# Turning C and B by VectorE's 32x32 transposes for three of six chunks

## The chip, the cores and the metric

One core of one Trainium2 chip runs the whole program. The metric is device time in microseconds (us) of one execution. Engines are named as the profile names them: PE is TensorE, PEld its weight loads, DVE VectorE, ACT ScalarE, POOL GpSimd, and SP the engine that issues all DMAs here. All data are float32.

## The reference, cut to what matters

A state-space scan in chunks (4 batches, 8 heads, 768 tokens, head size 32, state size 16) is followed by a feed-forward block with a hard-swish.

```python
for c in range(nc):                                   # chunks of tokens
    cum = np.cumsum(la, axis=-1)                      # la = log of the decay a
    L = np.exp(cum[:, :, :, None] - cum[:, :, None, :]) * causal
    M = np.einsum('bhin,bhjn->bhij', Cc, Bc) * L
    y_intra = np.einsum('bhij,bhjd->bhid', M, xc)
    y_inter = np.einsum('bhin,bhnd->bhid', Cc, state) * np.exp(cum)[:, :, :, None]
    y[:, :, sl] = y_intra + y_inter
    Bx = np.einsum('bhjn,bhjd->bhjnd', Bc, xc) * decay_from_j[:, :, :, None, None]
    state = decay_full[:, :, None, None] * state + np.sum(Bx, axis=2)
# y as (3072, 256), then
h = y @ w_in                                          # 256 x 2048
g = h * np.clip(h + 3.0, 0.0, 6.0) / 6.0
return g @ w_out                                      # 2048 x 256
```

Both products of C, with B and with the state, contract over the state size n. On TensorE the contracted dimension lies on the partitions, so C and B, which come from memory with n innermost, are needed with n on the partitions. Getting them there is called turning.

## The kernel before

The kernel uses chunks of 128 tokens, six in all. Stage k = 0 to 5 computes the feed-forward block of chunk k while it prepares the scan of chunk c = k + 1 and loads chunk `ahead` = k + 2. The instructions of each engine run in the order in which the program writes them (a manual schedule), and SP's queue too. A tile that reuses a buffer waits until the readers of the old content are done.

Stages 1 to 5 have two halves on TensorE:

- The first product (y times `w_in`) runs in steps s = 0 to 7. Each step issues `early`, `lead` of the next step, `last` of the previous one and `middle` (all recorded at L490). ACT and DVE fetch the banks `odd` and `even`, form the ramp (L524, L529) and leave the result in `gT`. The function `lead` ends with an ACT copy (L503) and the DVE copy `up` (L504), and `middle` with two DVE additions (L516, L517). POOL sums quarters of `gT` (`g_sums`, L585) after s = 2, 4, 6 and at the start of the second half.
- The second product (`gT` times `w_out`, L599) is a chain of 14 units, i = 0 to 13, in two rounds t = 0 and 1. They collect in two banks, `oa` and `ob`, and DVE combines them (L624 after unit 10, L634 and L635 after unit 12, L640 after unit 13 for t = 1; L644 to L646 after unit 7 for t = 0). Between the units the scan of the next chunk is placed: `scores` (products of C and B at L376, times L on DVE at L384) after units 2 and 4, `results` (`mix` on TensorE at L400, L409, L417, then `keep`, which copies y on ACT at L432 and updates the state on DVE) after units 4 and 7, `sum_y` (DVE, L487) after unit 7, and `lead` of the next stage after unit 12. ACT's exponentials of chunk `ahead` (L312, and `from_start`, L315, for the table `eto`) run after units 2 to 6.

Turning a chunk takes two calls of `turn`, each for two batches. In stages 1 to 4 they stand in the first product, after steps s = 3 and s = 5. Each call has four TensorE transposes of 128x128 into one PSUM bank `t_ps` (L343), an ACT copy that takes B out as `bT` (L347), a DVE product that takes C out twice, masked by the head's parity, as `cT` (L359), and a DVE product with the decay from the chunk's start, `eto`, as `csT` (L365). In stage 0 chunk 1 is turned, and chunk 0 before that.

In `load`, SP brings C and B of a chunk as tokens by heads (L85) and x (L92), three issues at the start of a stage. `rows` brings the cumulated log decays for chunk `ahead` + 1 after unit 7: four issues for L (L247), which POOL masks in `conceal` (L303), and eight for `eto` (L253), one for each head, which land in 16 partitions each. B by tokens is also multiplied by the decay to the chunk's end (`ends`, POOL, L323). The scan's decay from chunk to chunk is applied by `carry` (POOL, L331).

Of the kernel before, what the change touches and what calls it, by code (L numbers as in the profile page):

```python
# [8 lines left out]
FP32 = mybir.dt.float32  # L9
# [3 lines left out]
AF = mybir.ActivationFunctionType  # L13
ALU = mybir.AluOpType
# [6 lines left out]
def kernel(  # L21
# [23 lines left out]
    nc = tc.nc  # L45
    P = 128
# [3 lines left out]
    NC = S // P  # L50
# [25 lines left out]
    a_sb = pre[:G, 0:2].rearrange("g t i -> g (t i)")[:, :S]  # L76
    nc.sync.dma_start(out=a_sb, in_=a.rearrange("b h s -> (b h) s"))

    loaded = {}

    def load_bc(c):
        sl = slice(c * P, (c + 1) * P)
        bc = loads.tile([P, 2, NB * NH, N], FP32, name="bc")
        for j, src in enumerate((C, B)):
            nc.sync.dma_start(  # L85
                out=bc[:, j], in_=src[:, :, sl, :].rearrange("b h s n -> s (b h) n"))
        loaded[c] = bc

    def load_x(c):
        sl = slice(c * P, (c + 1) * P)  # L90
        xt = loads.tile([P, NB * NH, D], FP32, name="xt")
        nc.sync.dma_start(out=xt, in_=x[:, :, sl, :].rearrange("b h s d -> s (b h) d"))  # L92
        loaded[c] = loaded[c], xt

    w_in = const.tile([P, NK, DF], FP32, name="w_in")
    w_sum = const.tile([P, NF // 2, P], FP32, name="w_sum")
# [152 lines left out]

    def load_eto(c):  # L250
        eto = att.tile([P, NB, P], FP32, name="eto")
        for h in range(NH):
            nc.sync.dma_start(  # L253
                out=eto[h * N:(h + 1) * N],
                in_=cum_d[c, h:NB * NH:NH].unsqueeze(0).to_broadcast([N, NB, P]))
        etos[c] = eto

    cum_n = const.tile([P, NC, G], FP32, name="cum_n")
# [58 lines left out]
    def ends(c, b):  # L317

        if c < NC - 1:
            if b == 0:  # L320
                bss[c] = att.tile([P, G, N], FP32, name="bs")
            hs = slice(b * NH, b * NH + NH)
            nc.gpsimd.tensor_tensor(  # L323
                out=bss[c][:, hs], in0=loaded[c][0][:, 1, hs],
                in1=decays_of(c, b)[:, :, P - 1:P].to_broadcast([P, NH, N]), op=ALU.mult)

    def carry(c):

        if c < NC - 1:
# [2 lines left out]
                out=tmps[c], in0=states[c - 1],  # L332
                in1=etos[c][:, :, P - 1:P].to_broadcast([P, NB, 2 * D]), op=ALU.mult)

    def turn(c, p):


        bc, xt = loaded[c]
        pool, tag = (ps, "f") if c < 2 else (ps_o, "o")
        t_ps = pool.tile([P, 4, P], FP32, name="t_ps", tag=tag)  # L340
        for k in range(4):
            j, b = k // 2, 2 * p + k % 2
            nc.tensor.transpose(  # L343
                out=t_ps[:, k],
                in_=bc[:, j, b * NH:(b + 1) * NH].rearrange("s h n -> s (h n)"), identity=ident)
        bT = att.tile([P, 2, P], FP32, name="bT")
        nc.scalar.copy(out=bT, in_=t_ps[:, 2:4])  # L347
        if c == 1 and p == 0:
            from_start(c)
            carry(c)  # L350
            for b in range(NB):
                ends(c, b)
        cT = att.tile([P, 2, 2, P], FP32, name="cT")
        if c == 1 or (c, p) == (0, 1):
            for t in range(2):
                nc.scalar.activation(
                    cT[:, :, t], t_ps[:, 0:2], AF.Copy, scale=parity[:, t:t + 1])
        else:
            nc.vector.tensor_tensor(  # L359
                out=cT, in0=t_ps[:, 0:2].unsqueeze(2).to_broadcast([P, 2, 2, P]),  # L360
                in1=parity.unsqueeze(1).unsqueeze(3).to_broadcast([P, 2, 2, P]), op=ALU.mult)
        csT = None
        if c:
            csT = att.tile([P, 2, P], FP32, name="csT")
            nc.vector.tensor_tensor(  # L365
                out=csT, in0=t_ps[:, 0:2], in1=etos[c][:, 2 * p:2 * p + 2], op=ALU.mult)
        bTs[c, p] = bT, cT, csT

    def scores(c, bs):

        bT, cT, csT = bTs[c, bs[0] // 2]
        cbs = [ps.tile([P, 2, 2, P], FP32, name="cb", tag="f") for q in range(NQ)]
        for b in bs:
            for q in range(NQ):
                rows = slice(32 * q, 32 * q + 32)
                nc.tensor.matmul(  # L376
                    out=cbs[q][:, b % 2].rearrange("j h i -> j (h i)"), lhsT=bT[rows, b % 2],
                    rhs=cT[rows, b % 2].rearrange("n t i -> n (t i)"), start=(b == bs[0]),
                    stop=True, tile_position=(32 * q, 0), skip_group_check=True)
        in_pair = slice(bs[0] % 2, bs[-1] % 2 + 1)  # L380
        L = Ls[c, bs[0] // 2][:, in_pair]
        for q in range(NQ):
            hs = slice(2 * q, 2 * q + 2)
            nc.vector.tensor_tensor(  # L384
                out=L[:, :, hs], in0=L[:, :, hs], in1=cbs[q][:, in_pair], op=ALU.mult)

    def mix(c, bs):


        xt = loaded[c][1]  # L390
        if bs[0] % 2 == 0:
            y_pss[c] = [ps_y.tile([P, 4, P], FP32, name=f"y{u}", tag=f"y{u}") for u in range(NK)]
        y_ps = y_pss[c]
        if c:

            for b in bs:
                csT = bTs[c, b // 2][2]
                for q in range(NQ):
                    rows, d0 = slice(32 * q, 32 * q + 32), 2 * D * (q % 2)
                    nc.tensor.matmul(  # L400
                        out=y_ps[q // 2][d0:d0 + 2 * D, b % 2], lhsT=states[c - 1][rows, b],
                        rhs=csT[rows, b % 2], start=(b == bs[0]), stop=True,
                        tile_position=(32 * q, d0), skip_group_check=True)
        for b in bs:
            L = decays_of(c, b)
            for u in range(NK):
                for q in range(HU):
                    h = HU * u + q
                    nc.tensor.matmul(  # L409
                        out=y_ps[u][32 * q:32 * q + 32, b % 2], lhsT=xt[:, b * NH + h],  # L410
                        rhs=L[:, h], start=(c == 0), stop=True, tile_position=(0, 32 * q),
                        skip_group_check=True)
        if c < NC - 1:
            for b in bs:
                for q in range(NQ):
                    hs = slice(b * NH + 2 * q, b * NH + 2 * q + 2)
                    nc.tensor.matmul(  # L417
                        out=y_ps[0][32 * q:32 * q + 32, 2 + b % 2, 0:2 * D],
                        lhsT=bss[c][:, hs].rearrange("s h n -> s (h n)"),
                        rhs=xt[:, hs].rearrange("s h d -> s (h d)"),  # L420
                        start=True, stop=True, tile_position=(0, 32 * q), skip_group_check=True)
# [232 lines left out]
    def rows(c):  # L654
        for b in range(NB):
            load_decay(c, b)
        load_eto(c)
# [91 lines left out]
    for k in range(NC):  # L749
# [56 lines left out]
        for s in range(NJ):  # L806
            early(k, s)
            if s == 0:
                if ahead < NC:
                    load(ahead)  # L810
                if c < NC:
                    carry(c)
            if s < NJ - 1:
                lead(k, s + 1)
            if s:
                last(k, s - 1)
                ramp(k, 2 * s - 2, evens[k, s - 1])
            middle(k, s)
            if s:
                times_ramp(k, 2 * s - 2, evens[k, s - 1])  # L820
            ramp(k, 2 * s + 1, odds[k, s])
            times_ramp(k, 2 * s + 1, odds[k, s])
            if s in (1, 3) and ahead < NC:
                conceal(ahead, s - 1)
                conceal(ahead, s)
            if s in (3, 5) and c < NC:
                turn(c, s // 4)
            if s in (2, 4, 6):
                g_sums(k, s - 2)
        for i, _ in enumerate(out_units(k)):  # L830
            if i == 0:
                s = NJ - 1
                last(k, s)
                ramp(k, 2 * s, evens[k, s])
                times_ramp(k, 2 * s, evens[k, s])
                g_sums(k, s - 1)
                if k == 1:
                    next(sums)
            if c < NC:
                if i in (2, 4):  # L840
                    if i == 4:
                        results(c, 0)
                    scores(c, ((0, 1), (2, 3))[i // 4])
                if ahead < NC and i in (2, 3, 5, 6):
                    decay_ends(ahead, {2: 0, 3: 1, 5: 2, 6: 3}[i])
                    if i == 6:
                        from_start(ahead)
                if i == 7:
                    results(c, 1)
                    sum_y(c)  # L850
                    if ahead + 1 < NC:
                        rows(ahead + 1)
                if i == 12:
                    lead(c, 0)

# [29 lines left out]
```

## Time and profile before

| | |
|---|---|
| median of 8 runs | 370.8 us (369.96 to 371.91) |
| the profiled execution | 370.13 us, of it 368.4 us span |
| granted TensorE clock, mean | 0.999 |
| PE busy | 360.4 us, 2893 instructions |
| DVE busy | 228.9 us, 448 instructions |
| ACT busy | 190.2 us, 414 instructions |
| POOL busy | 134.5 us, 134 instructions |
| TensorE transposes into `t_ps` (L343) | 48, 273 ns in the record |
| `bT` copies (L347, ACT) | 12, 366 ns |
| `cT` on DVE (L359) | 9, 685 ns |
| `csT` on DVE (L365) | 10, 417 ns |
| C issues (L85), 256 KB | 6, 5.4 us to landing |
| B issues (L85), 256 KB | 6, 7.7 us to landing |
| `eto` issues (L253), 32 KB | 40, 5.1 us to landing |

The span runs from the first to the last instruction; the execution's own time is a little longer. Busy time of PE is that of pipelined instructions whose ends are modelled, so the distance of the starts of two neighbours says more than the duration of one. A group's line gives line of code, engine, operation and tiles (out<-in), then count, busy time and mean time of one. In an order of time, a line begins with the start in us from the span's start and the busy us; what stands in brackets at its end is the idle time before it and what ended that.

### The profile page before, as it was taken

Reading aid. Unit: us, or ns where it says so; the run is one execution under the profiler, and the core shown is the slowest. Engines: PE = TensorE matmul, PEld = TensorE weight load, DVE = VectorE, ACT = ScalarE, POOL = GpSimd, SP = SyncE. Lnnn points to the kernel's source line nnn. Section 1 sums busy time; section 2 is a strip of 40 time slices with the busy share of each in tenths; the row PEclk is TensorE's granted clock in tenths of the full one; section 3 lists DMA queues with packets and bytes.
Section 4 is the critical chain, followed back from the end, with each engine's and each line's share of the span. In section 5 each row is a group of like instructions: output and inputs, shape, how many; then the busy total and the mean of one; then the engine's idle time right before and its main releaser. Section 6 shows DMA issues by size and latency. Waiting matters only on the chain.

```text
span 368.4 us, 7275 instructions
## 1 busy us (share of the span) xinstructions
PE 360.4 (98%) x2893; PEld 306.5 (83%) x2893; DVE 228.9 (62%) x448; ACT 190.2 (52%) x414; POOL 134.5 (37%) x134
## 2 busy tenths in 40 slices
PE   7899999999999999999999999999999999999996
PEld 3564468778888999888899888999888989888996
DVE  7779999894896632786452688343488342488111
ACT  5867878765674831674750575570466100366100
POOL 1200020631499412099512088600058800057800
PEclk9999999999999999999999999999999999999999
DMA  9968999703790036900027930000000000000000
GB/s 165 201 228 181 186 355 119 240 5 81 237 113 3 2 117 195 114 6 2 3 68 223 106 34 0 2 24 8 28 3 1 2 2 30 28 1 2 2 28 28
DMA packets 86689, 29.21 MB, mean 79 GB/s; under 512 B 75456, under 2 KB 81248, under 8 KB 86656
## 3 DMA queue, kind: packets, MB, share of 16 engines
q1 hardware_dynamic: 86656, 28.76, 38.2%
q8 instruction: 22, 0.36, 0.5%
q14 instruction: 11, 0.09, 0.1%
HBM read 25.53 MB, written 3.23 MB: 78 GB/s over the span
## 4 chain that ended last, share of the span: by engine, by line
PE 82%; DVE 8%; ACT 6%; DMA 2%; issue 1%; SPq 0%; ACTq 0%
PE even L490 19%; PE ob L599 17%; PE oa L599 17%; PE odd L490 14%; PE cb L376 4%; PE y L409 3%; PE o L540 3%; DVE gT L529 2%; DVE wm L178 2%; ACT we L175 2%; PE y L400 2%; DMA raw<-in_moe_w_in_dram 2%; ACT L L312 1%; ACT L L298 1%; PE t_ps L343 1%; DVE w_out L191 1%
## 5 line engine op out<-in xcount | busy, mean ns | idle before, releaser
L585 POOL TENSOR_TENSOR s<-gT 128x512 f32<-128x512 f32 x20 | 26.4, 1320 | 104.0 <-DVE gT L529 104.0
L490 PE MATMUL even<-ts,w_sum 128*128 128x256 f32 x160 | 48.2, 383 | 0.0
L524 ACT ACTIVATE gT<-odd,half 128x512 f32<-128x512 f32 x40 | 27.5, 687 | 35.5 <-DVE odd L517 35.5
L503 ACT COPY even<-odd 128x512 f32<-128x512 f32 x40 | 23.0, 575 | 43.0 <-PE odd L490 42.0
L312 ACT ACTIVATE L<-L,cum_n 128x128 f32<-128x128 f32 x144 | 43.2, 392 | 2.1 <-POOL L L303 2.1
L490 PE MATMUL odd<-yT,w_in 128*128 128x256 f32 x160 | 41.1, 379 | 0.0
L384 DVE TENSOR_TENSOR L<-L,cb 128x512 f32<-128x512 f32 (+1 forms) x56 | 30.3, 605 | 17.2 <-PE cb L376 17.2
L599 PE MATMUL oa<-w_out,gT 128*128 128x128 f32 x320 | 39.3, 278 | 0.0
L599 PEld LDWEIGHTS oa<-w_out,gT 128*128 128x128 f32 x320 | 38.1, 192 | 1.4 <-issue 0.2
L303 POOL TENSOR_SCALAR_AFFINE_SELECT L<-L 128x1024 f32<-128x1024 f32 x18 | 20.1, 1131 | 49.7 <-DMA L<-cum_d 49.6
L599 PE MATMUL ob<-w_out,s 128*128 128x128 f32 x320 | 37.8, 276 | 0.0
L599 PEld LDWEIGHTS ob<-w_out,s 128*128 128x128 f32 x320 | 36.5, 192 | 1.3 <-issue 1.3
L490 PEld LDWEIGHTS even<-ts,w_sum 128*128 128x128 f32 x160 | 29.9, 190 | 5.3 <-ACT up L510 1.5
L529 DVE SCALAR_TENSOR_TENSOR gT<-gT,odd 128x512 f32<-128x512 f32 x40 | 27.5, 687 | 9.9 <-ACT gT L524 9.8
L490 PEld LDWEIGHTS odd<-yT,w_in 128*128 128x128 f32 x160 | 30.1, 190 | 3.9
L524 ACT ACTIVATE gT<-even,half 128x512 f32<-128x512 f32 x40 | 27.8, 695 | 4.4 <-PE even L490 4.4
L529 DVE SCALAR_TENSOR_TENSOR gT<-gT,even 128x512 f32<-128x512 f32 x40 | 27.2, 679 | 4.4 <-ACT gT L524 4.4
L599 PE MATMUL ob<-t,gT 128*128 128x128 f32 x240 | 29.7, 277 | 0.0
L599 PEld LDWEIGHTS ob<-t,gT 128*128 128x128 f32 x240 | 28.0, 192 | 1.3 <-issue 1.3
L540 PE MATMUL o<-w_out,gT 128*128 128x256 f32 x128 | 28.9, 381 | 0.0
L504 DVE COPY up<-odd 128x256 f32<-128x256 f32 x40 | 16.9, 423 | 18.3 <-ACT even L503 14.4
L448 PE MATMUL h<-yT,w_in 128*128 128x512 f32 x64 | 27.7, 594 | 0.0
(110 smaller groups left out, 629.7 us busy)
## 6 DMA issues: line engine op xcount, KB each, us to landing
L<-cum_d SPq DMA_DIRECT2D x18, 512.0 KB, 6.8
raw<-in_moe_w_in_dram SPq DMA_DIRECT2D x4, 1024.0 KB, 8.5
raw<-in_moe_w_out_dram SPq DMA_DIRECT2D x4, 1024.0 KB, 8.8
xt<-in_x_dram SPq DMA_DIRECT2D x6, 512.0 KB, 8.6
out_dram<-res SPq DMA_DIRECT2D x20, 128.0 KB, 1.7
bc<-in_C_dram SPq DMA_DIRECT2D x6, 256.0 KB, 5.4
bc<-in_B_dram SPq DMA_DIRECT2D x6, 256.0 KB, 7.7
eto<-cum_d SPq DMA_DIRECT2D x40, 32.0 KB, 5.1
```

Of the source, the lines that this page charges most:

```text
L303: nc.gpsimd.affine_select(out=L, in_=L, pattern=[[0, NH], [1, P]], compare_op=ALU.is_ge, fill=-1e5, base=0, channel_multiplier=-1)
L312: nc.scalar.activation(L[:, h], L[:, h], AF.Exp, bias=cum_n[:, c, g:g + 1])
L384: nc.vector.tensor_tensor(out=L[:, :, hs], in0=L[:, :, hs], in1=cbs[q][:, in_pair], op=ALU.mult)
L448: nc.tensor.matmul(out=h.rearrange("p r i -> p (r i)"), lhsT=w_in[:, j, f * P:(f + 1) * P], rhs=yTs[k][:, j].rearrange("p b i -> p (b i)") ...
L490: nc.tensor.matmul(out=bank[:, r], lhsT=lhsT, rhs=rhs, start=start, stop=True, skip_group_check=True)
L503: nc.scalar.copy(out=even, in_=odd[:, 1:2].to_broadcast([P, 2, 2 * P]))
L504: nc.vector.tensor_copy(out=up[:, 1], in_=odd[:, 0])
L524: nc.scalar.activation(gTs[k][:, f], h.rearrange("p r i -> p (r i)"), AF.Relu, bias=half, scale=1.0 / 6.0)
L529: nc.vector.scalar_tensor_tensor(out=g, in0=g, scalar=1.0, in1=h.rearrange("p r i -> p (r i)"), op0=ALU.min, op1=ALU.mult)
L540: nc.tensor.matmul(out=o[:, b % 2], lhsT=gTs[0][:, f, b * P:(b + 1) * P], rhs=w_out[:, f], start=(f == 0 and b % 2 == 0), stop=True, skip_ ...
L585: nc.gpsimd.tensor_tensor(out=o, in0=p_, in1=q_, op=op)
L599: nc.tensor.matmul(out=bank[:, slot], lhsT=lhs[:, j], rhs=rhs[:, j], start=(clear and j == 0), stop=True, skip_group_check=True)
```

## The change

For chunks 3, 4 and 5 (`TURN = 3`), C and B are loaded a second way. Each partition holds one pair of heads and one group of four tokens, and its elements lie as head of the pair, batch, token of the group, state index. This takes eight issues of 32 KB for each of C and B, one for each batch and head of a pair. A block of 32 partitions and 32 elements then is 32 token groups by (head, state index), so a 32x32 transpose puts head and state index on the partitions and the tokens along the free dimension. The function `turn_all` turns the whole chunk by two such transposes on DVE, masks C twice by parity (two scalings of 128x512) and multiplies it by `eto`. It stands after unit 9 of the second product, for chunk `ahead`, so in stages 1, 2 and 3. The calls of `turn` in stages 2, 3 and 4 fall away. B by tokens is still loaded, for `ends`; C by tokens is not loaded for these chunks.

The tiles `bT`, `cT` and `csT` now hold a whole chunk, in one buffer each where there were two. The pair tiles of C and B share the two buffers of the old C tile.

For all chunks, `load_eto` has four issues, one for each batch, over all 128 partitions, instead of eight over 16 partitions each.

```diff
     def load_bc(c):
         sl = slice(c * P, (c + 1) * P)
-        bc = loads.tile([P, 2, NB * NH, N], FP32, name="bc")
-        for j, src in enumerate((C, B)):
-            nc.sync.dma_start(
-                out=bc[:, j], in_=src[:, :, sl, :].rearrange("b h s n -> s (b h) n"))
-        loaded[c] = bc
+        def tokens_first(src, **where):
+            t = loads.tile([P, NB * NH, N], FP32, **where)
+            nc.sync.dma_start(out=t, in_=src[:, :, sl, :].rearrange("b h s n -> s (b h) n"))
+            return t
+
+        def pairs_first(src):
+            t = loads.tile([P, 2, NB, 4, N], FP32, name="pairs", tag="bc")
+            for b in range(NB):
+                for h in range(2):
+                    nc.sync.dma_start(
+                        out=t[:, h, b].rearrange("s a n -> s (a n)"),
+                        in_=src[b, h:NH:2, sl, :].rearrange("h (s a) n -> h s (a n)", a=4))
+            return t
+
+        if c < TURN:
+            bcs[c] = [tokens_first(C, name="C", tag="bc")]
+        Bs[c] = tokens_first(B, name="B")
+        if c < TURN:
+            bcs[c].append(Bs[c])
+        else:
+            bcs[c] = [pairs_first(C), pairs_first(B)]
...
     def load_eto(c):
         eto = att.tile([P, NB, P], FP32, name="eto")
-        for h in range(NH):
+        for b in range(NB):
             nc.sync.dma_start(
-                out=eto[h * N:(h + 1) * N],
-                in_=cum_d[c, h:NB * NH:NH].unsqueeze(0).to_broadcast([N, NB, P]))
+                out=eto[:, b],
+                in_=cum_d[c, b * NH:(b + 1) * NH].unsqueeze(1).to_broadcast([NH, N, P]))
         etos[c] = eto
...
+    def turned(c):
+        if c not in bTs:
+            bTs[c] = [att.tile([P, 2, 2, P], FP32, name="bT", bufs=1),
+                      att.tile([P, 2, 2, 2, P], FP32, name="cT", bufs=1),
+                      att.tile([P, 2, 2, P], FP32, name="csT", bufs=1) if c else None]
+        return bTs[c]
...
+    def turn_all(c):
+
+        bT, cT, csT = turned(c)
+        for t, out_ in zip(bcs[c], (csT, bT)):
+            nc.vector.transpose(
+                out=out_.rearrange("r p b (s a) -> r (p b) a s", a=4),
+                in_=t.rearrange("s t b a n -> s (b a) t n"))
+        for t in range(2):
+            nc.vector.tensor_scalar(
+                out=cT[:, :, :, t].rearrange("r p b i -> r (p b) i"),
+                in0=csT.rearrange("r p b i -> r (p b) i"), scalar1=parity[:, t:t + 1],
+                scalar2=None, op0=ALU.mult)
+        nc.vector.tensor_tensor(
+            out=csT, in0=csT, in1=etos[c].rearrange("r (p b) i -> r p b i", p=2), op=ALU.mult)
...
-            if s in (3, 5) and c < NC:
+            if s in (3, 5) and c < TURN:
                 turn(c, s // 4)
...
+                if i == 9 and TURN <= ahead < NC:
+                    turn_all(ahead)
                 if i == 12:
                     lead(c, 0)
```

More of the change, by code (lines that the diff above doesn't have):

```diff
@@ L77 @@
     nc.sync.dma_start(out=a_sb, in_=a.rearrange("b h s -> (b h) s"))
-    loaded = {}
+    Bs, bcs, xts = {}, {}, {}
+    TURN = 3
     def load_bc(c):
         sl = slice(c * P, (c + 1) * P)
-        bc = loads.tile([P, 2, NB * NH, N], FP32, name="bc")
-        for j, src in enumerate((C, B)):
-            nc.sync.dma_start(
-                out=bc[:, j], in_=src[:, :, sl, :].rearrange("b h s n -> s (b h) n"))
-        loaded[c] = bc
+        def tokens_first(src, **where):
[17 more added lines that the diff above has]
+            bcs[c] = [pairs_first(C), pairs_first(B)]
     def load_x(c):
         sl = slice(c * P, (c + 1) * P)
-        xt = loads.tile([P, NB * NH, D], FP32, name="xt")
-        nc.sync.dma_start(out=xt, in_=x[:, :, sl, :].rearrange("b h s d -> s (b h) d"))
-        loaded[c] = loaded[c], xt
+        xts[c] = loads.tile([P, NB * NH, D], FP32, name="xt")
+        nc.sync.dma_start(out=xts[c], in_=x[:, :, sl, :].rearrange("b h s d -> s (b h) d"))
     w_in = const.tile([P, NK, DF], FP32, name="w_in")
@@ L323, in ends @@
             nc.gpsimd.tensor_tensor(
-                out=bss[c][:, hs], in0=loaded[c][0][:, 1, hs],
+                out=bss[c][:, hs], in0=Bs[c][:, hs],
                 in1=decays_of(c, b)[:, :, P - 1:P].to_broadcast([P, NH, N]), op=ALU.mult)
@@ L333, in carry @@
                 in1=etos[c][:, :, P - 1:P].to_broadcast([P, NB, 2 * D]), op=ALU.mult)
+    def turned(c):
[4 more added lines that the diff above has]
+        return bTs[c]
     def turn(c, p):
-        bc, xt = loaded[c]
+        bT, cT, csT = turned(c)
         pool, tag = (ps, "f") if c < 2 else (ps_o, "o")
@@ L344, in turn @@
                 out=t_ps[:, k],
-                in_=bc[:, j, b * NH:(b + 1) * NH].rearrange("s h n -> s (h n)"), identity=ident)
-        bT = att.tile([P, 2, P], FP32, name="bT")
-        nc.scalar.copy(out=bT, in_=t_ps[:, 2:4])
+                in_=bcs[c][j][:, b * NH:(b + 1) * NH].rearrange("s h n -> s (h n)"),
+                identity=ident)
+        nc.scalar.copy(out=bT[:, p], in_=t_ps[:, 2:4])
         if c == 1 and p == 0:
@@ L352, in turn @@
                 ends(c, b)
-        cT = att.tile([P, 2, 2, P], FP32, name="cT")
         if c == 1 or (c, p) == (0, 1):
@@ L356, in turn @@
                 nc.scalar.activation(
-                    cT[:, :, t], t_ps[:, 0:2], AF.Copy, scale=parity[:, t:t + 1])
+                    cT[:, p, :, t], t_ps[:, 0:2], AF.Copy, scale=parity[:, t:t + 1])
         else:
             nc.vector.tensor_tensor(
-                out=cT, in0=t_ps[:, 0:2].unsqueeze(2).to_broadcast([P, 2, 2, P]),
+                out=cT[:, p], in0=t_ps[:, 0:2].unsqueeze(2).to_broadcast([P, 2, 2, P]),
                 in1=parity.unsqueeze(1).unsqueeze(3).to_broadcast([P, 2, 2, P]), op=ALU.mult)
-        csT = None
         if c:
-            csT = att.tile([P, 2, P], FP32, name="csT")
             nc.vector.tensor_tensor(
-                out=csT, in0=t_ps[:, 0:2], in1=etos[c][:, 2 * p:2 * p + 2], op=ALU.mult)
-        bTs[c, p] = bT, cT, csT
+                out=csT[:, p], in0=t_ps[:, 0:2], in1=etos[c][:, 2 * p:2 * p + 2], op=ALU.mult)
+    def turn_all(c):
+        bT, cT, csT = turned(c)
+        for t, out_ in zip(bcs[c], (csT, bT)):
[9 more added lines that the diff above has]
+            out=csT, in0=csT, in1=etos[c].rearrange("r (p b) i -> r p b i", p=2), op=ALU.mult)
     def scores(c, bs):
-        bT, cT, csT = bTs[c, bs[0] // 2]
+        bT, cT = (t[:, bs[0] // 2] for t in bTs[c][:2])
         cbs = [ps.tile([P, 2, 2, P], FP32, name="cb", tag="f") for q in range(NQ)]
@@ L387, in mix @@
     def mix(c, bs):
-        xt = loaded[c][1]
+        xt = xts[c]
         if bs[0] % 2 == 0:
@@ L396, in mix @@
             for b in bs:
-                csT = bTs[c, b // 2][2]
+                csT = bTs[c][2][:, b // 2]
                 for q in range(NQ):
```

## The prediction

> **What bounds the kernel now.** I read four views in this order: the busy shares of the page, busy time by stage, TensorE's order of time around the transposes, and VectorE's order of time where the new block goes.
>
> First a line of the page's first part, then two tables by stage. Their windows run from one "early" product of a stage to that of the next: stages k = 2, 3, 4, then k = 5 to the end. Each line has the length, then busy us and instruction count of each engine.
>
> ```profile
> PE 360.4 (98%) x2893; PEld 306.5 (83%) x2893; DVE 228.9 (62%) x448; ACT 190.2 (52%) x414; POOL 134.5 (37%) x134
> ```
>
> ```profile
> 145.72:202.74 57.02, 1.20 (x8) 1.00 (x8) 2.03 (x4) 0.73 (x2) 1.00 0.35 70
> ...
> 316.34:368.40 52.06, 0.00 (x0) 0.00 (x0) 0.00 (x0) 0.00 (x0) 0.99 0.04 13
> ```
>
> ```profile
> 202.74:259.76 57.02, 57.02 (x506) 51.70 (x505) 32.16 (x68) 29.13 (x72) 22.03 (x18) 1.00 0.25 30
> 259.76:316.34 56.58, 56.58 (x474) 51.05 (x473) 31.21 (x64) 19.25 (x39) 19.99 (x16) 1.00 0.03 11
> ```
>
> The columns are PE, PEld, DVE, ACT (and POOL), then granted clock, DMA share and GB/s. The second fence counts only instructions that touch `t_ps`; the third counts all. See: in stages 3 and 4 TensorE is busy for the whole stage at granted clock 1.00, and each stage still sends 8 transposes through it. DVE is busy for 56%. So work taken off TensorE there is time, and work given to DVE is free while it fits in a hole.
>
> TensorE in stage 4 (start, us, then instructions merged):
>
> ```profile
> 270.46 0.59 PE L490 MATMUL odd<-ts,w_in 128*128 128x256 f32 x2
> 270.89 0.59 PE L490 MATMUL even<-ts,w_sum 128*128 128x256 f32 x2
> 271.32 0.60 PE L343 MATMUL t_ps<-ident,bc 128*128 128x128 f32 x4
> 271.76 0.60 PE L490 MATMUL even<-yT,w_in 128*128 128x256 f32 x2
> ...
> 281.70 0.59 PE L490 MATMUL even<-ts,w_sum 128*128 128x256 f32 x2
> 282.25 0.70 PE L490 MATMUL even<-yT,w_sum 128*128 128x256 f32 x2
> ```
>
> See: the record says 273 ns for a transpose, but they are pipelined. What four of them cost is the distance of starts, 271.76 - 271.32 = 0.44 us. At the end of this first product the distance is 282.25 - 281.70 = 0.55 where it is 0.43 everywhere else. In stage 5, which turns nothing, the same pair stands 0.43 apart (337.40 and 337.83). So a stage that turns also has 0.12 us of wait.
>
> VectorE around the end of stage 2, the second place where the new block goes:
>
> ```profile
> 192.50 0.66 DVE L487 TENSOR_TENSOR yT<-yT 128x256 f32<-128x256 f32 x1
> 193.07 0.87 DVE L487 TENSOR_TENSOR ts<-yT,ts 128x256 f32<-128x256 f32 x2
> 196.56 0.42 DVE L624 TENSOR_TENSOR res<-oa,x 128x256 f32<-128x256 f32 x1 [2.61 <-DMA L<-cum_d]
> 200.13 0.42 DVE L634 TENSOR_TENSOR u<-ob,res 128x256 f32<-128x256 f32 x1 [3.15 <-PE ob L599]
> ```
>
> See: after `sum_y` (L487) DVE is idle 2.61 us, and 3.15 us more after `res`. The block stands between L487 and L624.
>
> **The change, part by part.** Sums are against the profiled execution: 370.13 us, of which 368.4 is span. The median of the runs shown is 370.8, so I add 0.67 at the end.
>
> *Transposes removed.* Chunks 3, 4 and 5 were turned in stages 2, 3 and 4, at steps s = 3 and 5: 2 x 0.44 = 0.88 us a stage. Check, by the same two groups of even products in the chain of waits: stage 4's first product takes 281.00 - 261.93 = 19.07, stage 5's 336.69 - 318.50 = 18.19; the difference is 0.88. Three stages: 2.64 us. The 0.12 wait is 0.36 over three stages. Bounds: nothing of it (it comes from something other than the turn), or all. I take 0.16, since stage 5 also lacks other work. Gain: 2.8 us.
>
> *Copies removed.* Per chunk, two `bT` copies on ACT (0.366 each), two `cT` (0.685) and two `csT` (0.417) on DVE. They are off TensorE's path, as the 0.88 shows: it is transposes alone. Their only worth is the 0.12 already taken.
>
> *The DVE block added, one per chunk in stages 1, 2 and 3 after unit 9.* Two 32x32 transposes of 128x512 f32 have no row. Nearest: a DVE operation over 128x512 f32, 0.682 (L384) to 0.687 (L529). Below: 0.41, the TENSOR_SCALAR over 32x512 f32 (L216), if a transpose also does two elements at a time. Above: 4 x 0.69 = 2.8 us, if a transpose of 4-byte elements with its writes 16 bytes apart took four passes. I take 0.69, as a single stream of 512 elements. Two scalings SBUF to SBUF: 0.41 each by L216. One product with `eto`: 0.69. Sum 2 x 0.69 + 2 x 0.41 + 0.69 = 2.9 us. Room: DVE is free at 193.95. What TensorE needs first is L624: it reads bank `oa`, which TensorE writes again at 200.79 (unit 13). So L624 must start by about 200.3, a room of 6.3 us. Behind it wait L634, L635 and `up` (L504, at 201.60), whose reader L516 comes at 205.45; these are looser. Cost: zero, hidden by units 10 to 12; without that cover it would be 2.9 x 3 = 8.7 us.
>
> Here a rule speaks against the change. Row: `yT<-yT` took 0.66 us at 192.50 in stage 2, while a POOL operation ran 192.19 to 192.87, and 0.43 in stage 3 with POOL idle. The Trainium skill, "SBUF — State Buffer", section "SBUF: two separate sides", says that VectorE (two SBUF inputs, or a two-port mode) and GpSimd hold a shared port pair exclusively for a whole instruction and the loser blocks. `conceal` (L303, 1.09 us each) runs at 195.65 and 198.28, inside the hole. By the row's 0.23 the block is 3.2; by the rule at most 2 x 1.09 more, so 5.1. Both are under 6.3. I take zero cost, but the margin by the rule is only 1.2 us.
>
> *Waits the block adds.* It needs `eto` after `from_start`: ACT ended that at 188.41, before `sum_y`. It overwrites `csT`, `cT` and `bT` of the chunk before, last read by the mix of unit 7 (TensorE, to 190.97), for which `sum_y` already waits. No added wait. Its result is first read a stage later.
>
> *Transfers of the pairs.* Per chunk of 3 to 5 the one C transfer goes, sixteen of 32 KB come, B by tokens stays. SP issues take 0.43 (C) or 0.30 to 0.86 (eto), so 16 cost 5 to 14 us of SP. In stages 2 and 3 they start near 146.6 and 203.6; SP's next work is at 190.08 in stage 2, so nothing waits behind but `x`, which is read a stage later. In stage 1 the B half reuses the buffer of chunk 2's C, so SP waits for that chunk's last transposes (106.74), with eight issues and `x` behind it; SP's next work is at 133.06. Landing: C and B of 256 KB land 5.4 and 7.7 us from issue, both inside 8.2. The Trainium skill, "DMA: Bandwidth & Descriptors", section "Why a DMA increments its semaphore by 16 and not by 1", says a transfer uses as many engines (16 at most) as divide the slowest dimension of both sides; here that is 4 heads against 128 partitions, so 4 engines. By the row: landed about 12 us after the first issue, with issue bound. By the rule: 4 x 8.2 = 33 us, plus some 3 us for B, so near 183 in stage 2, with DVE there at 193.95. In stage 1: half of it, 107 + 17 = 124 against 136.9. Zero by both; by the rule the cover is 11 to 13 us.
>
> *The decay table.* Eight issues become four, same bytes, chunks 1 to 5: SP is freed by 4 x 0.43 or more each time. The tightest reader is chunk 2's: issued 64.6 to 73.5, used on ACT at 86.64, and ACT's copy for the first lead follows it. Bounds: 0.3 us won (the one wait for a w_out load, 0.68, is in that stretch) or 0.5 lost. I take zero.
>
> *POOL.* The sum that unit 4 needs (`s2`) ends at 176.46; TensorE reads it at 178.72. With TensorE 1.0 us earlier, 1.3 us is left. Zero.
>
> Sum: 370.13 - 2.8 = 367.3, plus 0.67: 368.0.
>
> **Rivals.** *A: as summed.* 368.0, own range 367.0 to 369.4 (a DVE delay taking up to half the gain back).
>
> *B: the gain is eaten.* TensorE arrives early and waits for what did not move: POOL's sums, or ACT's exponentials before the `yT` copies (2.62 us idle at 191.03). Against it: 1.3 and 1.6 us of slack would be left. For it: POOL is slowed if DVE locks it out. Time: 370.0 to 371.5, near 370.8.
>
> *C: slower, the block holds DVE's queue.* Place: L624 behind the two transposes. If each takes 2.8 us the block is 5.6 + 1.5 = 7.1, and with `conceal` in the way 9.3. Past 6.3, each us is a us of TensorE at unit 13: 0.8 to 3.0 a stage. At 3.0 in stages 1 and 2 and 0.8 in stage 3: 6.8 - 2.8 = +4.0, so 374.8. It decides for slower once the block passes 6.3 + 2.8/3 = 7.2 us in every stage, which is 2.9 us a transpose (1.8 with the port). For it: no row of such a transpose. Against: every f32 DVE row over 512 elements from one stream is 0.4 to 0.7.
>
> *D: the change does not get TensorE off the turning, or the pairs come late.* The first would leave L343 at 48 instructions; the diff guards `turn` by `c < TURN`, so no. The second needs landings over 47 us.
>
> **How the numbers follow.** A 0.77, B 0.09, C with D's second half 0.14. A measurement here can tell about 0.3%, 1.1 us, from no change. A lies beyond it, so faster 0.77, same 0.09, slower 0.14. The range, 367.0 to 371.0, holds A and the nearer part of B.
>
> **What would show it.** L343 falls from 48 to 24. Stages 2, 3 and 4 fall from 57.02, 57.02, 56.58 to about 56.1, 56.1, 55.7, stages 1 and 5 staying within 0.2. A new DVE group of 6 transposes near 0.7 us starts at about 136.9 (stage 1), with L624 about 0.5 to 1.5 us later than now and L634 where it was relative to TensorE. L347 falls to 6. It would be wrong if PE shows idle at unit 13, or DVE waits for a transfer ahead of the transposes.

## The result and the profile after

The changed kernel takes 367.41 us in the median (367.04 to 369.2), the kernel before in the same comparison 370.38 us (369.9 to 372.1). The ratio is 0.9918, with a 95% interval of 0.9904 to 0.9932, so it is faster by about 3.0 us. The profiled execution took 368.2 us, of it 366.5 us span. One execution further down, of a kernel with VectorE's copies put back, ran at a granted clock of 0.56 and took 616.07 us, so its stages are not used; in the stages compared, k = 1 to 4, the clock was 1.00.

Here are the tables by stage of both kernels. Their windows run from one stage's first `early` product to the next's, for k = 1 to 5. Each line has the length, then busy us and count of PE, PEld, DVE, ACT and POOL, then clock, DMA share and GB/s. Before:

```profile
88.06:145.56 57.50, 57.47 (x506) 51.46 (x505) 33.61 (x69) 29.70 (x73) 29.68 (x27) 1.00 0.51 113
145.56:202.58 57.02, 57.02 (x507) 51.70 (x505) 32.39 (x68) 29.12 (x72) 26.51 (x25) 1.00 0.34 68
202.58:259.60 57.02, 57.02 (x506) 51.70 (x505) 32.16 (x68) 29.13 (x72) 22.03 (x18) 1.00 0.26 31
259.60:316.18 56.58, 56.58 (x475) 51.05 (x473) 31.21 (x64) 19.25 (x39) 19.99 (x16) 1.00 0.03 11
316.18:368.40 52.22, 48.92 (x334) 45.33 (x332) 22.89 (x48) 16.83 (x32) 19.95 (x16) 0.99 0.04 13
```

After:

```profile
88.87:146.33 57.46, 57.46 (x506) 51.46 (x505) 37.79 (x74) 29.69 (x73) 29.74 (x27) 1.00 0.47 118
146.33:202.35 56.02, 56.02 (x498) 50.92 (x497) 34.76 (x69) 28.57 (x70) 27.04 (x25) 1.00 0.34 76
202.35:258.37 56.02, 56.02 (x498) 50.92 (x497) 33.72 (x69) 28.58 (x70) 21.99 (x18) 1.00 0.21 34
258.37:313.95 55.58, 55.58 (x467) 50.27 (x466) 29.46 (x60) 18.70 (x37) 19.97 (x16) 1.00 0.03 11
313.95:366.50 52.55, 48.92 (x334) 45.33 (x332) 22.89 (x48) 16.84 (x32) 19.96 (x16) 1.00 0.04 13
```

Stages 2, 3 and 4, the three that no longer turn, are 1.00 us shorter each. Stage 1 still turns chunk 2 and is as before (57.50 and 57.46), although it now holds a DVE block too (DVE 37.79 us there). That makes 3.00 us, the whole gain by stages. These two spans differ by only 1.9 us, for two reasons. The last window is 0.3 us longer in the changed kernel. That is not chance: up to the last VectorE instruction stage 5 takes 48.96 us in both, and from there to the end it takes 3.5 to 3.6 us in every profile of a kernel with the new decay table, and 3.3 us in the two with the old one. So the table costs 0.2 to 0.3 us there; why is not shown. The other reason is that the profiled execution of the changed kernel came to stage 1 0.81 us later. This is not the change's: in a second profile of the changed kernel stage 1 began at 88.21. The late start shows in the first matmuls. Changed kernel, TensorE's order of time:

```profile
6.64 0.63 PE L311 MATMUL d<-less,split 128*128 128x512 bf16 x1
7.07 0.63 PE L308 MATMUL d<-split,pick 128*128 128x128 bf16 x4
```

The same place in the kernel before:

```profile
6.37 0.38 PE L292 MATMUL d<-less,split 128*128 128x512 bf16 x1
6.59 0.39 PE L289 MATMUL d<-split,pick 128*128 128x128 bf16 x4
```

The starts are 0.43 us apart in one and 0.22 in the other. Both executions begin with 0.43 (from 2.3 us on) and change to 0.22, one at 11.6 us and the other at 6.4. The trace's records of the granted clock begin just before, at 11.35 and at 5.68 us; for the time without a record the tables print 1.00, so a 1.00 in the first microseconds says nothing. The Trainium skill, "TensorE: Matmul & The Clock Gate", section "Wait — 56ns, not 53.3ns?", gives 426.7 ns for a 512-column matmul on a cold array and 215.7 on a warm one, and the distances agree. Since the moment of the change differs from execution to execution, I compare lengths of stages below, and times only where they say more.

VectorE at the end of stage 2, changed kernel:

```profile
192.84 0.87 DVE L524 TENSOR_TENSOR ts<-yT,ts 128x256 f32<-128x256 f32 x2
194.01 1.11 DVE L395 STREAM_TRANSPOSE csT<-pairs 128x512 f32<-128x512 f32 x1 [0.30 <-issue]
194.97 1.10 DVE L395 STREAM_TRANSPOSE bT<-pairs 128x512 f32<-128x512 f32 x1
195.90 0.81 DVE L399 TENSOR_SCALAR cT<-csT,parity 128x512 f32<-128x512 f32 x2
196.74 1.46 DVE L403 TENSOR_TENSOR csT<-csT,eto 128x512 f32<-128x512 f32 x1
198.12 0.41 DVE L661 TENSOR_TENSOR res<-oa,x 128x256 f32<-128x256 f32 x1
199.90 0.42 DVE L671 TENSOR_TENSOR u<-ob,res 128x256 f32<-128x256 f32 x1 [1.37 <-PE ob L636]
```

The block fills the hole of 2.61 us after `sum_y` and part of the next one. Of the 3.15 us that VectorE was idle before L634 (now L671), 1.37 us is left, and L671 still waits for TensorE. No transfer stands before the block.

### The profile page after: what moved, and what is told of

It reads as the page before. It is cut to its first block, busy times and chain, and to the rows that moved or that the text cites. A ratio compares the mean times of both kernels' runs of the same rounds, so it can differ in the third digit from the quotient of the medians.

```text
span 366.5 us, 7245 instructions
## 1 busy us (share of the span) xinstructions
PE 359.6 (98%) x2869; PEld 305.8 (83%) x2869; DVE 234.4 (64%) x451; ACT 189.2 (52%) x408; POOL 135.3 (37%) x134
## 4 chain that ended last, share of the span: by engine, by line
PE 80%; issue 10%; DMA 5%; SPq 3%; POOL 1%; DVE 0%; POOLq 0%
PE even L527 19%; PE ob L636 17%; PE oa L636 17%; PE odd L527 14%; PE o L577 3%; PE cb L413 3%; DMA B<-in_B_dram 3%; PE y L446 3%; DMA L<-cum_d 2%; PE y L437 2%; SPq L266 1%; SPq L112 1%; POOL L L322 1%; SPq L89 1%; POOL bs L342 1%
```

## The experiments

Stage lengths in us, k = 1 to 4. The changed kernel is the line to compare with.

| kernel | k = 1 | k = 2 | k = 3 | k = 4 | median time |
|---|---|---|---|---|---|
| before | 57.50 | 57.02 | 57.02 | 56.58 | 370.38 |
| changed | 57.46 | 56.02 | 56.02 | 55.58 | 367.41 |
| changed, again | 57.42 | 56.03 | 56.03 | 55.57 | 367.36 |
| transposes back | 57.51 | 56.90 | 56.91 | 56.45 | 370.05 |
| one transpose, all copies back | 57.41 | 57.18 | 57.18 | 56.73 | 371.25 |
| one transpose, DVE's copies back | 57.42 | 57.19 | 57.18 | 56.78 | 370.92 |
| copies from `odd` back | 57.46 | 58.24 | 58.24 | 57.86 | 374.22 |
| block with 4 transposes | 57.52 | 56.03 | 56.02 | 55.58 | 367.95 |
| block with 8 transposes | 60.15 | 58.65 | 58.35 | 55.58 | 375.02 |
| old decay table | 57.43 | 56.03 | 56.02 | 55.58 | 367.71 |
| chunk 2 too | 56.87 | 56.02 | 56.02 | 55.58 | 367.14 |
| chunk 2 too, split | 56.46 | 56.03 | 56.02 | 55.58 | 366.31 |

**Transposes back.** My theory was that the gain is TensorE's own time for the transposes. The rival was that it is the relief of VectorE and ScalarE.

```diff
             if s in (3, 5) and c < TURN:
                 turn(c, s // 4)
+            if s in (3, 5) and TURN <= c < NC:
+                idle_turn(c, s // 4)      # four TensorE transposes into t_ps, no reader
```

> The changed kernel with the 24 TensorE transposes put back in stages 2 to 4 after steps 3 and 5, into a bank that nobody reads (the result still comes from VectorE). Theory 1 (the gain is TensorE's own time, 0.44 us a call, and the other 0.12 us a stage was the copies' lag on VectorE and ScalarE): stages 2 to 4 at 56.90, 56.90, 56.46, the run about 2.6 us above the changed kernel, near 370.0. Theory 2 (the 0.12 too is TensorE's): stages at 57.02, 57.02, 56.58, 3.0 us above. Theory 3 (the gain is mainly VectorE's and ScalarE's relief in the first product): under 1 us above.

The first `early` products of its stages 4 and 5:

```profile
260.74 0.60 PE L536 MATMUL even<-yT,w_in 128*128 128x256 f32 x2
317.19 0.60 PE L536 MATMUL even<-yT,w_in 128*128 128x256 f32 x2
```

The stages grew by 0.88, 0.89 and 0.87 us, just theory 1. So four transposes cost 0.44 us of TensorE, and the other 0.12 us of a turning stage is there only when the copies are too. This does not say that the copies are worth no more than that.

**Copies back, first try.**

```diff
+            if s in (3, 5) and TURN <= c < NC:
+                idle_copies(c, k, s)      # ACT 128x256, DVE 128x512 and 128x256, out of odd
```

> The changed kernel with copies of the sizes of turn's put back in stages 2 to 4 after steps 3 and 5 (one 128x256 on ScalarE, one 128x512 and one 128x256 on VectorE, from a bank already there into an unread tile), without any TensorE work. Theory 1: only the 0.12 us a stage come back, stages at 56.14, 56.14, 55.70, the run 0.4 us above the changed kernel. Theory 2: nothing comes back, within 0.1 us. Theory 3: over 1.5 us above.

Each stage grew by 2.2 us. The run does not answer the question, because these copies wait as those of `turn` never did: ScalarE's for VectorE's `gT`, VectorE's for ScalarE's. They read the bank `odd` and write one tile; which of the two makes the waits is not shown. The waits of the tile of these copies:

```profile
  DVE gT L579: 4.5, 6
  ACT spare L394: 2.6, 6
```

**Copies back, with a bank of their own.** One transpose fills the bank, so that the copies wait for TensorE alone, as in `turn`.

```diff
+            if s in (3, 5) and TURN <= c < NC:
+                idle_turn(c, s // 4)
+    def idle_turn(c, p):                  # t_ps as in turn; spare is read by nobody
+        nc.tensor.transpose(out=t_ps[:, 0], in_=..., identity=ident)
+        nc.scalar.copy(out=spare[:, 0], in_=...)             # 128x256
+        nc.vector.tensor_tensor(out=spare, in0=..., in1=...)     # 128x512, by parity
+        nc.vector.tensor_tensor(out=spare[:, 1], in0=..., in1=...)   # 128x256, by eto
```

> The changed kernel with, in each of the six places of stages 2 to 4, one TensorE transpose (not four) and the three copies of turn behind it in turn's order (ScalarE 128x256, VectorE 128x512 and 128x256, into an unread tile). Theory 1 (the copies by themselves cost the 0.12 us a stage): stages at 0.22 + 0.12 above the changed kernel's, 56.36, 56.36, 55.92, the run about 1.0 us above. Rival (the copies were hidden because the four transposes gave VectorE 0.44 us more in the same step; a step without them is 3.02 us against some 3.7 us of VectorE work): 0.6 to 1.5 us a stage, the run 2 to 4.5 us above.

The first `early` products of its stages 4 and 5:

```profile
260.70 0.60 PE L541 MATMUL even<-yT,w_in 128*128 128x256 f32 x2
317.43 0.60 PE L541 MATMUL even<-yT,w_in 128*128 128x256 f32 x2
```

The stages grew by 1.16, 1.16 and 1.15 us: the rival. With one transpose for four, a stage is even 0.16 us longer than before the change. The waits of TensorE's weight loads follow, with their sum, their number and the longest, and then the place in stage 4. Stages 2, 3 and 4 have one wait of 1.2 us each there:

```profile
PEld even L541 <- DVE odd L568: 4.5, 6, 1.2
```

```profile
282.14 0.59 PE L541 MATMUL even<-ts,w_sum 128*128 128x256 f32 x2
283.50 0.70 PE L541 MATMUL even<-yT,w_sum 128*128 128x256 f32 x2 [0.77 <-DVE odd L568]
```

This is the pair that stood 0.55 us apart before the change and now stands 1.36 apart. VectorE is behind by then. VectorE around the second set of copies, first in this run:

```profile
280.49 0.69 DVE L580 SCALAR_TENSOR_TENSOR gT<-gT,odd 128x512 f32<-128x512 f32 x1 [0.17 <-ACT gT L575]
281.10 0.68 DVE L398 TENSOR_TENSOR spare<-t_ps,parity 128x512 f32<-128x512 f32 x1
281.81 0.42 DVE L401 TENSOR_TENSOR spare<-t_ps,eto 128x256 f32<-128x256 f32 x1
282.16 0.41 DVE L555 COPY up<-odd 128x256 f32<-128x256 f32 x1
282.49 0.42 DVE L567 TENSOR_TENSOR odd<-odd,up 128x256 f32<-128x256 f32 x1
283.01 0.43 DVE L568 TENSOR_TENSOR odd<-even,up 128x256 f32<-128x256 f32 x1
```

The same place in the kernel before:

```profile
279.97 0.69 DVE L359 TENSOR_TENSOR cT<-t_ps,parity 128x512 f32<-128x512 f32 x1
280.57 0.42 DVE L365 TENSOR_TENSOR csT<-t_ps,eto 128x256 f32<-128x256 f32 x1
280.90 0.42 DVE L504 COPY up<-odd 128x256 f32<-128x256 f32 x1
281.23 0.42 DVE L516 TENSOR_TENSOR odd<-odd,up 128x256 f32<-128x256 f32 x1
281.76 0.43 DVE L517 TENSOR_TENSOR odd<-even,up 128x256 f32<-128x256 f32 x1
```

The copies stand ahead of `up`, L567 and L568, and TensorE's `last` waits for L568. Counted from the start of stage 4, the second addition (L517, here L568) began at 22.16 us before the change, at 21.16 in the changed kernel, at 22.04 with the transposes alone and at 22.32 here. Stage 4 is longer than in the changed kernel by the same amounts, to 0.01 us. The 0.16 us between this run and the kernel before is mostly the experiment's own: its two copies start 0.71 us apart and the ones of `turn` 0.60. Here both write `spare`, there two tiles; that this is the reason is not shown.

**Only VectorE's copies.** To see which engine held it up, ScalarE's copy was taken out again.

```diff
-        nc.scalar.copy(out=spare[:, 0], in_=t_ps[:, 0:1].to_broadcast([P, 2, P]))
```

> As the run with one transpose and three copies in each place, but without the ScalarE copy: one transpose and VectorE's 128x512 and 128x256 operations. If VectorE's 1.1 us a place made the 1.16 us a stage, stages 2 to 4 stay at about 57.1, 57.1, 56.7. If ScalarE's copy, which stands ahead of its up copy, made it, they fall to about 56.3, 56.3, 55.9 (0.22 of transposes and a little wait).

Its other times (370.3 us and up) equal those of the run with all copies. The stages come from one more execution of the same kernel.

> The kernel with one transpose and VectorE's two copies in each place, once more, for a profile at full clock. Its times before (370.3 and up) equal those of the run with ScalarE's copy as well, so stages 2 to 4 are expected at 57.1 to 57.2, 57.1 to 57.2 and 56.7, with TensorE waiting for the additions behind the copies at the end of each first product; 56.3, 56.3, 55.9 would mean that ScalarE's copy made it.

They are 57.19, 57.18 and 56.78, with the same 4.5 us of waits for the addition. So it is VectorE's two copies, 1.1 us a place, and not ScalarE's.

**Block with 4 and with 8 transposes.** How much room does the block have, and what ends it?

```diff
-        for t, out_ in zip(bcs[c], (csT, bT)):
+        for t, out_ in 2 * list(zip(bcs[c], (csT, bT))):     # 4 * for the second kernel
```

> The changed kernel with the two VectorE transposes of the block done twice (same result). The block grows by about 2.0 us, from 3.4 to 4.2 up to 5.4 to 6.2. If the room is the 6.3 us of the prediction (L661 before TensorE's unit 13), nothing is lost: within 0.2 us of the changed kernel. If VectorE's queue is already on the path, 1 to 2 us a stage, so 3 to 6 us above.

> The changed kernel with the two VectorE transposes done four times (same result), a block of about 9.2 to 10.0 us. Prediction's room of 6.3 us, set by bank oa at unit 13: TensorE waits about 2.9 us in stage 3 and 3.7 in stages 1 and 2 at unit 13, about 10 us above the changed kernel. Rival (the room is some 9 us, set by up and its readers in the next first product): under 2.5 us above, and no wait at unit 13.

With four transposes no stage grew by more than 0.06 us. With eight, stages 1 to 3 grew by 2.69, 2.63 and 2.33 us. Block with eight, stage 1, TensorE at unit 13, and then the waits of TensorE over the run:

```profile
142.49 1.03 PE L527 MATMUL odd<-yT,w_in 128*128 128x256 f32 x4
145.88 2.05 PE L636 MATMUL oa<-t,gT 128*128 128x128 f32 x16 [2.37 <-DVE res L661]
```

```profile
PE oa L636 <- DVE res L661: 6.8, 3, 2.4
```

VectorE began the block at 136.45 and L661 at 145.41, 8.96 us later. With a room of 6.3 us that is 2.66 us too much in stage 1, and 2.69 was measured; in stage 2 it is 2.66 against 2.63. Unit 13 itself came 2.5 us late: it began 3.39 us after the products at 142.49, where it is 0.86 in the changed kernel.

In stage 3 the block took 8.89 us, so the room of 6.3 gives 2.59, and 2.33 was measured; the hole is 0.24 us longer there (2.85 us before L624 in the kernel before), which the prediction had not counted. The unit, the bank and the reader are those of the prediction. The sizes said before the run (2.9 and 3.7 us) were too large, because the block was expected at 9.2 to 10.0 us: `conceal` fell beside the transposes this time and stretched them little (1.15 us at most).

**Dense transposes.** Why did a transpose take 1.11 us?

```diff
-            nc.vector.transpose(
-                out=out_.rearrange("r p b (s a) -> r (p b) a s", a=4),
-                in_=t.rearrange("s t b a n -> s (b a) t n"))
+            if out_ is csT:               # C: dense writes
+                nc.vector.transpose(
+                    out=out_.rearrange("r p b (a s) -> r (p b) a s", a=4),
+                    in_=t.rearrange("s t b a n -> s (b a) t n"))
+            else:                         # B: dense on both sides
+                nc.vector.transpose(
+                    out=out_.rearrange("r p b (a s) -> r (p b a) s", a=4),
+                    in_=t.rearrange("s t b a n -> s (t b a n)").rearrange("s (m f) -> s m f", f=32))
```

> The changed kernel with dense accesses in the two VectorE transposes, which leaves the tokens (and in the second the heads) in another order than needed: the first writes without the step of four elements, the second reads and writes without a step. If the step of the writes made a transpose 1.1 us instead of 0.69, the first or both now take 0.69. If a 4-byte transpose itself takes that long, both stay at 1.1.

```profile
L396 DVE STREAM_TRANSPOSE csT<-pairs x3: 711/711/712, 136.5 to 248.3; 128x512 f32<-128x512 f32 x3
L400 DVE STREAM_TRANSPOSE bT<-pairs x3: 669/669/671, 137.1 to 248.9; 128x512 f32<-128x512 f32 x3
```

The columns in ns are least, median and most. This kernel leaves the tokens in another order than the products need, so only the durations are read from it. Dense writes bring 1.11 down to 0.71, dense reads beside them to 0.67. So the writes with a step of four elements cost 0.40 us, and the 4-byte transpose itself runs like the other operations over 128x512 f32 from one stream (0.68 to 0.69).

**The old decay table.**

```diff
-        for b in range(NB):
+        for h in range(NH):               # eight issues over 16 partitions, as before
...
```

> The changed kernel with the decay table loaded as before, eight issues over 16 partitions. Theory (the table is off the path on both sides): every stage within 0.1 us of the changed kernel, SP some 3 to 6 us longer at it, the run within 0.5 us. Rival (it wins part of the 3 us, through the start or stage 0): 0.5 to 1.5 us above.

No stage from 1 to 4 moved. SP's issues for the table of chunk 2 took 8.52 us instead of 2.49. From the first product of stage 0 to stage 1 this run shows 65.11 us and the kernel before 64.74. The nine profiles of kernels with the new table and the same stage 0 show 64.51 to 64.92, the changed kernel 64.52. So what the new table wins there lies between nothing and 0.6 us, and it loses 0.2 to 0.3 us at the end of the run. The medians, 367.71 and 367.41, do not decide the sum.

**Chunk 2 too.** If the hole at a stage's end takes the block, the end of stage 0 might take one for chunk 2.

```diff
-    TURN = 3
+    TURN = 2
@@ stage 0
                         rows(ahead)
+                        load_pairs(ahead)     # chunk 2's pairs, behind its rows
@@
                         lead(c, 0)
+                        turn_all(ahead)
```

> The changed kernel with chunk 2 turned by VectorE as well: its pairs are loaded in stage 0 behind the rows of chunk 2, the block stands at the end of stage 0 behind the first lead, where VectorE is idle 1.3, 3.0 and 0.8 us, and TensorE's eight transposes go from stage 1. Theory: stage 1 falls from 57.46 to about 56.5, stage 0 is up to 0.4 us longer, the run 0.5 to 1.0 us below the changed kernel. Rival (the block of 3.5 us or late pairs hold up the second up copy, or the transfers crowd stage 0): no gain, or 0.5 to 3 us above.

Stage 1 fell by 0.59, not by 1.0, and the median by 0.3 us: the block ran 87.65 to 91.02, the second `up` came 0.28 us late, and TensorE waited 0.26 us for the additions behind it. The theory had 0.5 to 1.0 us for the run; the hold-up that the rival named was real and took part of it.

**Chunk 2 too, split.**

```diff
                         turn_all(ahead)       # for chunk 2 the two transposes alone
@@ stage 1, step 0
             ramp(k, 2 * s + 1, odds[k, s])
+            if k == 1 and s == 0:
+                mask_and_decay(c, 0)          # the two scalings
             times_ramp(k, 2 * s + 1, odds[k, s])
@@ stage 1, after unit 1
+            if k == 1 and i == 1:
+                mask_and_decay(c, 1)          # the product with eto
```

> The run that turned chunk 2 on VectorE lost 0.26 us and more at the second even product, because the block of four instructions held up the second up copy by 0.28 us; stage 1 was 56.87. Here the block of chunk 2 is split: the two transposes stay at the end of stage 0, the two scalings go behind the first step's additions (0.75 us idle there), the product with the decay goes behind unit 1 of stage 1. If that hold-up was all, stage 1 is 56.46 to 56.6 and the run 0.8 to 1.0 us below the changed kernel. If the rest comes from elsewhere, stage 1 stays at 56.8 or more.

Stage 1 is 56.46, the full 1.00 below. The median is 366.31 us; the ratio to the kernel before is 0.9876 (0.9853 to 0.9899), while the changed kernel on the same chip had 0.990 (0.9877 to 0.9923), median 367.36. All five of its times (366.08 to 366.62) lie below all six of the changed kernel there (366.95 to 367.59). So this is the best version of these, 1.0 us below the changed kernel, although the two intervals against the kernel before overlap a little.

> The changed kernel itself, once more, for comparison on the same chip: stages 57.46, 56.02, 56.02, 55.58, and a ratio to the kernel before near 0.992.

## Why the prediction was right, point by point, and where not

**Time and stages.** 368.0 us was predicted and 367.41 measured. Of these 0.6 us, 0.4 is the base: the sum started from 370.8, and the kernel before had 370.38 in the comparison. The gain was put at 2.8 us and is 3.0. The transposes' 2.64 us came out as said (0.88 in each stage, by the transposes put back). The wait of 0.12 us a stage was entered at 0.16 in all and was worth its upper bound, 0.36; together that is the 3.00 of the stages.

**The step "Copies removed" failed, though the sum held.** It said that the copies are off TensorE's path, "as the 0.88 shows", and worth the 0.12 alone. They are on it as soon as the transposes are gone. A stage costs 0.88 us more with the transposes alone, 1.16 us with one transpose and VectorE's copies (some 1.0 without what is the experiment's own), and 1.00 us with all of both. TensorE's and VectorE's additions to a step lay side by side and were nearly the same size, and only the longer one counted. That was VectorE's: the 1.00 us of a turning stage is the delay of its second addition. The kernel with one transpose has taken away three quarters of TensorE's turning and gained nothing on the kernel before. So the comparison of stage 4 with stage 5, which lacks both, could not tell whose time it was. The change gained because it took both out of the first product at once. That the sum held was luck in this respect: by the prediction's reasoning, a change that took out the transposes and left the copies would have gained most of it, too.

**The block.** The prediction put a transpose at 0.69 us, and it took 1.11; the four-element step of its writes is the reason (dense: 0.71). Two neighbours overlap, though, and start 0.96 us apart. From its first start to L661's the block took 3.3 us in stage 3 instead of 2.9, and 4.1 in stages 1 and 2. The rival of slow transposes had allowed up to 2.8 each and named 6.3 us as the room; the run with eight transposes put the limit at unit 13, where it said, and the room within 0.3 us. The cover was right, and at 4.1 us some 2 us of it was left.

**The shared port.** In stages 1 and 2 `conceal` ran beside the block, in stage 3 it did not. First `conceal` in stages 1 and 2, then the scalings of stages 1 and 3 and the product of stage 3:

```profile
139.36 1.09 POOL L322 TENSOR_SCALAR_AFFINE_SELECT L<-L 128x1024 f32<-128x1024 f32 x1 [2.75 <-DMA L<-cum_d]
196.40 2.76 POOL L322 TENSOR_SCALAR_AFFINE_SELECT L<-L 128x1024 f32<-128x1024 f32 x2 [3.76 <-PE oa L636]
```

```profile
139.53 1.59 DVE L399 TENSOR_SCALAR cT<-csT,parity 128x512 f32<-128x512 f32 x2
251.35 0.80 DVE L399 TENSOR_SCALAR cT<-csT,parity 128x512 f32<-128x512 f32 x2
252.18 0.69 DVE L403 TENSOR_TENSOR csT<-csT,eto 128x512 f32<-128x512 f32 x1
```

The scalings took 1.59 us in stage 1 and 0.80 in stage 3, the product 1.46 us in stage 2 and 0.69 in stage 3. So the stretch was 0.8 us a stage, between the row's 0.23 and the 2.2 of the page's rule. It fell on the product, whose two inputs in SBUF the rule names, and on the scalings; that these run in the rule's two-port mode is not shown. It went both ways: the two `conceal` of stage 2 took 1.26 and 1.54 us instead of 1.09. The transposes were spared: with eight of them in stage 1, two `conceal` ran beside them, and the transposes took 1.06 to 1.11 us and `conceal` 1.09.

**Transfers.** SP took 0.54 us for most pair issues, so 11 to 14 us a chunk and not more. The C pairs of chunk 3 were issued from 96.20, the B pairs from 107.92, behind the last TensorE transposes of chunk 2, as said. No transfer is named before any block. The profile gives no landing for them, but the trace has the packets: 2048 of 256 bytes for each of these chunks, the last at 114.5, 160.4 and 216.5 us, 1.6 to 1.9 us after SP's last issue. So the transfers kept pace with the issues, as the prediction had it by the row (12 us after the first issue; 12.6 in stage 2), and its 183 us by the rule did not come. The number of engines need not be what was wrong: the trace has 64 packets of 4 bytes for the sixteen transfers of stage 1, four each, and sixteen for the B load of 256 KB, which fits the four engines of the rule. What did not hold is scaling the landing time of the 256 KB loads by four. The cover was 23 us in stage 1 and 34 in stage 2, not 11 to 13.

**Signs named beforehand.** TensorE's transposes are 24 and the `bT` copies on ScalarE 6. The first block begins at 137.64 (136.9 was said, before the late start). L624's place, now L661, is later against TensorE by 1.5, 1.8 and 0.4 us, where 0.5 to 1.5 was said. L634's place is where it was. TensorE did not wait at unit 13.

**The decay table.** It was entered at zero, between 0.3 us won and 0.5 lost in stage 0, and the medians show nothing else. The 0.2 to 0.3 us that it costs behind the last VectorE instruction had no term; up to 0.6 us won in stage 0 stands against it.

## What to carry to other kernels

When one engine is busy for the whole of a stage, the work that runs beside it is not free for that reason: if another engine's addition to the same step is as long, taking off the first alone gains little, and one has to put each back by itself to know. Before moving a block onto an engine that works in order, find the first instruction behind it that the bound engine needs, and count the idle time up to there; that number held here to 0.3 us. A block that almost fits can be cut at its instructions and spread over several holes.

## What the hardware showed that I had not expected

A 32x32 transpose of 128x512 f32 on VectorE took 1.06 to 1.15 us when its writes stepped by four elements (16 bytes), and 0.67 to 0.71 us with dense writes. GpSimd's selections did not slow it beyond that, while they stretched the scalings and the product beside them to twice their time. Every execution began with bf16 matmuls of 512 columns 0.43 us apart; in most the distance fell to 0.22 between 6.3 and 6.6 us, in two only at 11.5. In the changed kernel's profile, one of these two, stage 0 then began its products about 1 us later (24.35 us against 23.32 in the kernel before).
